# Banded ALiBi attention and a hard-swish MoE on one core: attention of the next batch interleaved with the MoE, masks on GpSimd

## The chip, the cores and the metric

The kernel runs on one core of one Trainium2 chip. The metric is the device time of one execution in microseconds, as the median of several runs. Lower is better.

## The reference, cut to what matters

Inputs are q, k and v of shape (8 batches, 8 heads, 576 positions, 64), and the weights w_in (512 x 2048) and w_out (2048 x 512), all float32.

```
scores = q @ k.T / 8
rel    = pos_q - pos_k
scores = where(0 <= rel < 128, scores - slope[h] * |rel|, -1e9)    # slope[h] = 2 ** -(h+1)
attn   = softmax(scores);  a = attn @ v
x      = a, heads side by side: (8 * 576 = 4608 tokens, 512)
h      = x @ w_in;  g = h * clip(h + 3, 0, 6) / 6;  out = g @ w_out
```

The band is 128 wide, so with tiles of 128 positions a block of queries meets two blocks of keys: its own (the diagonal block, masked on one side) and the one before it (the off-diagonal block, masked on the other side). 576 is four tiles of 128 and one of 64.

## The kernel before, in words

It runs in three stages, one after the other. First it builds 16 bias tiles of 128 x 128 (lines L58 to L77: a diagonal and an off-diagonal one for each head, with the ALiBi slope and a large negative number where the band ends) and loads the weights on SyncE's DMA queue (L86, L90), with a cast to bf16 on VectorE (L87, L91).

Then comes attention: a loop over 8 batches and 4 pairs of heads. For each pair and each of the 5 tiles of positions, six DMAs of 128 x 64 floats bring q, k and v of two heads (L111 to L113), VectorE scales and casts them (L114 to L124), TensorE transposes q and k of both heads together (L126, L128) and VectorE copies the results from PSUM (L127, L129). For each tile of queries and each head there are one or two score matmuls over 64 rows (L144); VectorE adds the bias tile in PSUM (L151), ScalarE takes exp (L153), TensorE multiplies with V (L155). V carries a column of ones, so the sum of the exps comes out beside the product; VectorE takes its reciprocal and multiplies (L160, L161). Both heads are transposed together (L165) and copied into xT (L166), which holds x transposed for all tokens.

Then comes the MoE, over 9 blocks of 512 tokens. In each, over 16 slices of the inner dimension: four matmuls of 512 columns give one 128 x 512 tile of h (L183), ScalarE takes Relu(h / 6 + 0.5) with a bias tile (L188), VectorE takes min with 1 and multiplies by h (L191), and four matmuls of 512 columns add to four output banks (L194). After the 16 slices VectorE copies the four banks out (L200) and SyncE stores them.

A planner of the tile framework orders each engine's instructions ahead of the run, by its own estimate of when operands and buffers are ready, with the program's order as priority. Each engine then runs its list strictly in that order, and a buffer is free again when its last reader is done. PSUM has eight banks; attention uses four kinds of tiles with two buffers each, the MoE four output banks and four banks for h.

## Time and profile before

| | before |
|---|---|
| median of 3 runs | 883.68 us (883.22 to 884.82) |
| profiled execution, span | 881.8 us |
| TensorE matmul busy | 595.5 us (68%) |
| VectorE busy | 577.0 us (65%) |
| ScalarE busy | 245.2 us (28%) |
| GpSimd busy | 5.1 us (1%) |
| DMA | 46.94 MB, 53 GB/s on average |

The profile shows one execution; its span goes from the first to the last instruction, and the time of the runs is 1.9 us above it. Matmuls are pipelined and their ends are modelled, so a busy time of TensorE counts overlapping matmuls' time once but is no measure of how densely they follow each other; start-to-start times are. "Idle before" is the time in which an engine had nothing to do, with the instruction that ended it.

### The profile page before, as it was taken

What the parts mean: (1) busy time and instruction counts of PE and PEld (TensorE: products, weight loads), DVE (VectorE), ACT (ScalarE), POOL (GpSimd) and SP (SyncE); (2) the same over time, 40 slices, a digit from 0 to 9 for tenths busy, and PEclk for the clock granted to TensorE, in tenths of its full rate; (3) what the DMA queues carried; (4) which work ended last, traced back from release to release, by engine and by line L of the source; (5) the groups of instructions that cost most, each with busy time, mean ns of one, the idle gap of its engine ahead of it and who ended that gap; (6) DMA issues with size and microseconds to landing.
All of it is one profiled execution on the core that took longest, in us unless ns stands there. A gap on an engine that the chain in (4) does not pass through costs nothing.

```text
span 881.8 us, 11904 instructions
## 1 busy us (share of the span) xinstructions
PE 595.5 (68%) x2760; PEld 262.3 (30%) x2784; DVE 577.0 (65%) x2939; ACT 245.2 (28%) x721; POOL 5.1 (1%) x24
## 2 busy tenths in 40 slices
PE   0155655565555555655566555555999999999996
PEld 0022222222222222222222222222334333343332
DVE  4577777777777777777777777775354435443543
ACT  0122222222222222222222222222334333433342
POOL 2000000000000000000000000000000000000000
PEclk9999999999999999999999999999999999999999
DMA  6522222222222222222222222221011001100111
GB/s 253 158 49 49 52 54 50 46 52 53 51 47 50 52 53 49 47 52 53 52 45 53 53 52 46 51 46 29 0 48 49 22 26 49 48 34 15 48 48 48
DMA packets 134085, 46.94 MB, mean 53 GB/s; under 512 B 126848, under 2 KB 126848, under 8 KB 133504
## 3 DMA queue, kind: packets, MB, share of 16 engines
q1 hardware_dynamic: 134016, 46.20, 20.2%
q8 instruction: 21, 0.34, 0.2%
q14 instruction: 48, 0.39, 0.2%
HBM read 36.70 MB, written 9.44 MB: 52 GB/s over the span
## 4 chain that ended last, share of the span: by engine, by line
PE 52%; DVE 25%; ACT 9%; issue 7%; DMA 5%; SPq 1%; DVEq 0%; POOL 0%; ACTq 0%; POOLq 0%
PE out_ps L194 15%; PE hT_ps L183 14%; DVE sc_ps L151 9%; ACT exp_sb L153 9%; PE av_ps L155 8%; PE sc_ps L144 6%; DVE qT L127 3%; PE avT_ps L165 3%; PE tps L128 3%; DVE xT L166 3%; PE tps L126 2%; DVE recip L160 2%; DVE vv L105 2%; DVE av_sb L161 2%; DMA tmp<-in_moe_w_out_dram 1%
## 5 line engine op out<-in xcount | busy, mean ns | idle before, releaser
L153 ACT ACTIVATE exp_sb<-sc_ps 128x128 bf16<-128x128 f32 (+1 forms) x576 | 145.0, 264 | 433.2 <-DVE sc_ps L151 364.7
L155 PE MATMUL av_ps<-vv,exp_sb 128*128 128x65 bf16 (+1 forms) x576 | 137.8, 242 | 176.8 <-ACT exp_sb L153 167.1
L151 DVE TENSOR_TENSOR sc_ps<-sc_ps,add_tiles 128x128 f32<-128x128 f32 (+1 forms) x576 | 154.3, 278 | 71.5 <-PE sc_ps L144 59.2
L191 DVE SCALAR_TENSOR_TENSOR gT<-r,hT_ps 128x512 bf16<-128x512 f32 x144 | 98.4, 686 | 141.6 <-ACT r L188 138.2
L144 PE MATMUL sc_ps<-qT,kT 64*128 64x128 bf16 (+1 forms) x576 | 139.2, 273 | 21.3 <-DVE qT L127 11.6
L188 ACT ACTIVATE r<-hT_ps,bias 128x512 f32<-128x512 f32 x144 | 98.9, 687 | 162.2 <-PE hT_ps L183 156.0
L155 PEld LDWEIGHTS <-exp_sb 128*128 128x128 bf16 (+1 forms) x576 | 63.1, 109 | 260.8 <-ACT exp_sb L153 238.9
L183 PE MATMUL hT_ps<-xT,w_in_sb 128*128 128x512 bf16 x565 | 138.9, 382 | 1.1 <-DVE xT L166 0.3
L194 PE MATMUL out_ps<-w_out_sb,gT 128*128 128x512 bf16 x563 | 138.2, 380 | 1.3 <-DVE gT L191 0.9
L161 DVE TENSOR_SCALAR av_sb<-av_ps,recip 128x64 bf16<-128x64 f32 (+1 forms) x320 | 88.3, 276 | 2.4
L183 PEld LDWEIGHTS <-w_in_sb 128*128 128x128 bf16 x576 | 56.8, 99 | 69.1 <-issue 2.2
L126 PE MATMUL tps<-ident,ldb 128*128 128x128 bf16 (+1 forms) x160 | 44.4, 278 | 45.2 <-DMA ldf<-in_k_dram 37.4
L194 PEld LDWEIGHTS <-gT 128*128 128x128 bf16 x576 | 46.4, 97 | 89.2 <-DVE gT L191 51.8
L160 DVE RECIPROCAL recip<-av_ps 128x1 f32<-128x1 f32 (+1 forms) x320 | 50.3, 157 | 33.7 <-PE av_ps L155 30.6
L144 PEld LDWEIGHTS <-kT 64*128 64x128 bf16 x576 | 53.1, 103 | 53.4 <-DVE kT L129 17.5
L128 PE MATMUL tps<-ident,ldb 128*128 128x128 bf16 (+1 forms) x160 | 42.2, 264 | 23.4 <-DVE qT L127 21.4
L165 PE MATMUL avT_ps<-ident,av_sb 128*128 128x128 bf16 (+1 forms) x160 | 44.5, 278 | 11.1 <-DVE av_sb L161 10.6
L166 DVE COPY xT<-avT_ps 128x128 bf16<-128x128 bf16 (+1 forms) x160 | 34.6, 216 | 12.3 <-PE avT_ps L165 8.2
L127 DVE COPY qT<-tps 128x128 bf16<-128x128 bf16 (+1 forms) x160 | 34.5, 216 | 9.9 <-PE tps L126 6.0
L129 DVE COPY kT<-tps 128x128 bf16<-128x128 bf16 (+1 forms) x160 | 34.1, 213 | 4.5 <-PE tps L128 0.5
L126 PEld LDWEIGHTS <-ldb 128*128 128x128 bf16 (+1 forms) x160 | 16.9, 106 | 56.1 <-DVE ldb L117 49.9
L128 PEld LDWEIGHTS <-ldb 128*128 128x128 bf16 (+1 forms) x160 | 16.6, 104 | 50.5 <-DVE ldb L121 38.9
(24 smaller groups left out, 255.7 us busy)
## 6 DMA issues: line engine op xcount, KB each, us to landing
out_dram<-osb SPq DMA_DIRECT2D x36, 256.0 KB, 2.1
ldf<-in_q_dram SPq DMA_DIRECT2D x256, 32.0 KB, 1.8
ldf<-in_k_dram SPq DMA_DIRECT2D x256, 32.0 KB, 1.8
ldf<-in_v_dram SPq DMA_DIRECT2D x256, 32.0 KB, 1.8
tmp<-in_moe_w_in_dram SPq DMA_DIRECT2D x4, 1024.0 KB, 7.8
tmp<-in_moe_w_out_dram SPq DMA_DIRECT2D x16, 256.0 KB, 3.4
ldf<-in_q_dram SPq DMA_DIRECT2D x64, 16.0 KB, 2.0
ldf<-in_k_dram SPq DMA_DIRECT2D x64, 16.0 KB, 2.0
```

The lines of the kernel that those rows point to most:

```text
L126: nc.tensor.transpose(tps[:, :sk], ldb[:sk, 0:2 * D], ident[:sk, :sk])
L128: nc.tensor.transpose(tps[:, :sk], ldb[:sk, 2 * D:4 * D], ident[:sk, :sk])
L144: nc.tensor.matmul(sc_ps[:sk, :sq], lhsT=kT[po:po + D, kslc], rhs=qT[po:po + D, qslc], start=True, stop=True)
L151: nc.vector.tensor_tensor(out=sc_ps[:sk, :sq], in0=sc_ps[:sk, :sq], in1=at, op=ALU.add)
L153: nc.scalar.activation(out=exp_sb[:sk, :sq], in_=sc_ps[:sk, :sq], func=ACT.Exp)
L155: nc.tensor.matmul(av_ps[:sq, :], lhsT=exp_sb[:sk, :sq], rhs=vv[_h][:sk, ds(kt_i * (D + 1), D + 1)], start=first_mm, stop=(kt_i == qt))
L161: nc.vector.tensor_scalar(out=av_sb[:sq, po:po + D], in0=av_ps[:sq, :D], scalar1=recip[:sq, :], scalar2=0.0, op0=ALU.mult, op1=ALU.add)
L165: nc.tensor.transpose(avT_ps[:, :sq], av_sb[:sq, :], ident[:sq, :sq])
L183: nc.tensor.matmul(hT_ps, lhsT=w_in_sb[:, ds(ks * d_ff + ms * 128, 128)], rhs=xT[:, ds(ks * Ntok + nt * NT, NT)], start=(ks == 0), stop=(k ...
L188: nc.scalar.activation(out=r6, in_=hT_ps, func=ACT.Relu, bias=bias3[:, 0:1], scale=1.0 / 6.0)
L191: nc.vector.scalar_tensor_tensor(out=gT, in0=r6, scalar=1.0, in1=hT_ps, op0=ALU.min, op1=ALU.mult)
L194: nc.tensor.matmul(out_ps[sub], lhsT=gT[:, ts(sub, 128)], rhs=w_out_sb[:, ts(ms, d_model)], start=(ms == 0), stop=(ms == n_ms - 1))
```

## The change

Attention is rebuilt and moved between the MoE's matmuls.

- Batch 0 is loaded first. The weights come by eight DMAs that GpSimd issues and that cast to bf16 on the way; nothing else casts them.
- A batch's q, k and v come by 15 DMAs (128 positions x 8 heads x 64), issued one batch ahead as buffers come free. GpSimd casts them to bf16.
- The ALiBi bias is split: within a block, exp(-slope * (q - k)) is a factor of the key, put in as exp's bias (one column per head, for diagonal and off-diagonal blocks), and a factor of the query, which cancels in the normalization. The 1/8 is exp's scale. The bias tiles are gone.
- Scores are taken for key tiles: two key tiles in one PSUM tile of two banks (one bank per head), 256 columns of queries for each, in two steps (`st`) per pair of heads; the second also has the fifth key tile. exp then runs on 256, 128 or 64 elements, and GpSimd zeroes what lies outside the band with affine_select on the exps.
- Normalizing and PSUM copies take whole groups: three reciprocals and three multiplies per pair, one copy of 576 columns per transposed operand.
- The MoE is split into two phases for each 512 tokens: `moe_up` writes all 16 slices of g, and `moe_down`, one block later, multiplies them with w_out, one output bank at a time.
- The main loop runs 10 stages of 16 steps. In stage nt each step has `moe_up` of block nt, `moe_down` of block nt - 1 and two or three of the 37 pieces of attention of batch nt + 1. Batch 0's attention stands alone ahead of the loop; stages 7 to 9 have no attention.

The core of the diff; the lines of the attention and MoE stages shown above are taken out, the sums of the normalization as before.

```diff
...
+    loads = ctx.enter_context(tc.tile_pool(name="loads", bufs=4))
+    casts = ctx.enter_context(tc.tile_pool(name="casts", bufs=2))
+    vpool = ctx.enter_context(tc.tile_pool(name="vpool", bufs=1))
+    qkt = ctx.enter_context(tc.tile_pool(name="qkt", bufs=3))
+    ppool = ctx.enter_context(tc.tile_pool(name="ppool", bufs=4))
+    small = ctx.enter_context(tc.tile_pool(name="small", bufs=4))
+    gpool = ctx.enter_context(tc.tile_pool(name="gpool", bufs=2))
+    rpool = ctx.enter_context(tc.tile_pool(name="rpool", bufs=3))
+    opool = ctx.enter_context(tc.tile_pool(name="opool", bufs=4))
+    ps_sc = ctx.enter_context(tc.tile_pool(name="ps_sc", bufs=1, space=bass.MemoryType.PSUM))
+    ps_av = ctx.enter_context(tc.tile_pool(name="ps_av", bufs=1, space=bass.MemoryType.PSUM))
+    ps_tp = ctx.enter_context(tc.tile_pool(name="ps_tp", bufs=2, space=bass.MemoryType.PSUM))
+    ps_h = ctx.enter_context(tc.tile_pool(name="ps_h", bufs=2, space=bass.MemoryType.PSUM))
+    ps_o = ctx.enter_context(tc.tile_pool(name="ps_o", bufs=1, space=bass.MemoryType.PSUM))
+
+    vbuf = [vpool.tile([128, NQ, H, W], BF16, name=f"vbuf{i}") for i in range(2)]
+    def load(b):
+        got = []
+        for src, nm in ((q, "qf"), (k, "kf"), (v, "vf")):
+            t = loads.tile([128, NQ, H, D], FP32, tag="ld", name=nm)
+            for j in range(NQ):
+                n = min(128, S - j * 128)
+                nc.sync.dma_start(
+                    out=t[:n, j, :, :],
+                    in_=src[b, :, ds(j * 128, n), :].rearrange("h p d -> p h d"))
+            got.append(t)
+        return got
+    first = load(0)
...
+    nc.gpsimd.iota(rel_i, pattern=[[0, 1]], base=0, channel_multiplier=1)
+    nc.vector.tensor_copy(out=rel_f, in_=rel_i)
+    for h in range(H):
+        nc.vector.tensor_scalar(out=bias_d[:, h:h + 1], in0=rel_f, scalar1=-64.0,
+                                scalar2=slopes[h], op0=ALU.add, op1=ALU.mult)
...
+    for ks in range(n_ks):
+        nc.gpsimd.dma_start(out=w_in_sb[:, ks, :], in_=moe_w_in[ts(ks, 128), :])
+    for g in range(4):
+        nc.gpsimd.dma_start(
+            out=w_out_sb[:, ts(g, 4), :],
+            in_=moe_w_out[ds(g * 512, 512), :].rearrange("(m p) d -> p m d", p=128))
+
+    def attention(b):
+        qf, kf, vf = first if b == 0 else load(b)
+        qb = casts.tile([128, NQ, H * D], BF16, name="qb")
+        kb = casts.tile([128, NQ, H * D], BF16, name="kb")
+        vb = vbuf[b % 2]
+        for src, dst in ((qf, qb), (kf, kb)):
+            s = src.rearrange("p j h d -> p j (h d)")
+            nc.gpsimd.tensor_copy(out=dst[:, 0:4, :], in_=s[:, 0:4, :])
+            nc.gpsimd.tensor_copy(out=dst[:LAST, 4, :], in_=s[:LAST, 4, :])
+        nc.gpsimd.tensor_copy(out=vb[:, 0:4, :, 0:D].rearrange("p j h d -> p (j h) d"),
+                              in_=vf[:, 0:4, :, :].rearrange("p j h d -> p (j h) d"))
+        nc.gpsimd.tensor_copy(out=vb[:LAST, 4, :, 0:D], in_=vf[:LAST, 4, :, :])
+        yield
+
+        for hp in range(NP):
+            qkT = []
+            for src, nm in ((qb, "qT"), (kb, "kT")):
+                tp = ps_tp.tile([128, S], BF16, tag="tp", name="tp")
+                for j in range(NQ):
+                    n = min(128, S - j * 128)
+                    nc.tensor.transpose(tp[:, ds(j * 128, n)], src[:n, j, ts(hp, 128)],
+                                        ident[:n, :n])
+                t = qkt.tile([128, S], BF16, tag=nm, name=nm)
+                nc.vector.tensor_copy(out=t, in_=tp)
+                qkT.append(t)
+                yield
+            qT, kT = qkT
+            pt = []
+            avs = small.tile([128, NQ, 2, D], BF16, tag="avs", name="avs")
+            for st in range(2):
+                sc = ps_sc.tile([128, 2, 512], FP32, tag="sc", name="sc")
+                for j in range(2):
+                    kt = 2 * st + j
+                    n = min(256, S - kt * 128)
+                    for e in range(2):
+                        nc.tensor.matmul(sc[:, e, ds(j * 256, n)],
+                                         lhsT=kT[e * D:(e + 1) * D, ts(kt, 128)],
+                                         rhs=qT[e * D:(e + 1) * D, ds(kt * 128, n)],
+                                         start=True, stop=True)
+                if st == 1:
+                    for e in range(2):
+                        nc.tensor.matmul(sc[:LAST, e, 448:512],
+                                         lhsT=kT[e * D:(e + 1) * D, 512:S],
+                                         rhs=qT[e * D:(e + 1) * D, 512:S],
+                                         start=True, stop=True)
+                pp = ppool.tile([128, 2, 2, 256], BF16, tag="p", name="pp")
+                p4 = None
+                if st == 1:
+                    p4 = ppool.tile([64, 2, 64], BF16, tag="p4", name="p4")
...
+                    s4 = sc[:, e, :].rearrange("p (j c) -> p j c", j=2)
+                    nc.scalar.activation(out=pp[:, e, :, 0:128], in_=s4[:, :, 0:128],
+                                         func=ACT.Exp, bias=bias_d[:, h:h + 1], scale=scale)
+                    if st == 0:
+                        nc.scalar.activation(out=pp[:, e, :, 128:256], in_=s4[:, :, 128:256],
+                                             func=ACT.Exp, bias=bias_o[:, h:h + 1], scale=scale)
...
+                dg = pp[:, :, :, 0:128].rearrange("p e j c -> p (e j) c")
+                nc.gpsimd.affine_select(out=dg, in_=dg, pattern=[[0, 4], [1, 128]],
+                                        channel_multiplier=-1, base=0,
+                                        compare_op=ALU.is_ge, fill=0.0)
...
+                pt.append(pp)
+                yield
+                qts = (0, 1) if st == 0 else (2, 3, 4)
+                nq = len(qts)
+                av = ps_av.tile([128, 3, 2, W], FP32, tag="av", name="av")
...
+                        if qt > 0:
+                            src = pt[(qt - 1) // 2][:, e, (qt - 1) % 2, 128:128 + m]
+                            nc.tensor.matmul(av[:m, i, e, :], lhsT=src, rhs=vb[:, qt - 1, h, :],
+                                             start=True, stop=False)
+                        if qt < 4:
+                            src = pt[qt // 2][:, e, qt % 2, 0:128]
+                            nc.tensor.matmul(av[:m, i, e, :], lhsT=src, rhs=vb[:, qt, h, :],
+                                             start=(qt == 0), stop=True)
...
+                    nc.vector.reciprocal(rc[:m, lo:lo + n, :, :], av[:m, lo:lo + n, :, D:W])
+                    nc.vector.tensor_tensor(
+                        out=avs[:m, qts[lo]:qts[lo] + n, :, :],
+                        in0=av[:m, lo:lo + n, :, 0:D],
+                        in1=rc[:m, lo:lo + n, :, :].to_broadcast([m, n, 2, D]),
+                        op=ALU.mult)
+                yield
+            tp = ps_tp.tile([128, S], BF16, tag="tp", name="tp")
+            for j in range(NQ):
+                n = min(128, S - j * 128)
+                nc.tensor.transpose(tp[:, ds(j * 128, n)],
+                                    avs[:n, j, :, :].rearrange("p e d -> p (e d)"), ident[:n, :n])
+            nc.vector.tensor_copy(out=xT[:, hp, ds(b * S, S)], in_=tp)
...
+    def moe_up(nt, ms):
+        if ms == 0:
+            gts[nt] = gpool.tile([128, n_ms, NT], BF16, tag="g", name="g")
+        hps = ps_h.tile([128, NT], FP32, tag="h", name="hps")
+        for ks in range(n_ks):
+            nc.tensor.matmul(hps, lhsT=w_in_sb[:, ks, ts(ms, 128)],
+                             rhs=xT[:, ks, ts(nt, NT)],
+                             start=(ks == 0), stop=(ks == n_ks - 1))
+        r6 = rpool.tile([128, NT], FP32, tag="r6", name="r6")
+        nc.scalar.activation(out=r6, in_=hps, func=ACT.Relu, bias=bias3[:, 0:1], scale=1.0 / 6.0)
+        nc.vector.scalar_tensor_tensor(out=gts[nt][:, ms, :], in0=r6, scalar=1.0, in1=hps,
+                                       op0=ALU.min, op1=ALU.mult)
+
+    def moe_down(nt, step):
+        sub, part = divmod(step, 4)
+        if part == 0:
+            ops[nt, sub] = ps_o.tile([128, d_model], FP32, tag="o", name="ops")
+        for i in range(4):
+            ms = part * 4 + i
+            nc.tensor.matmul(ops[nt, sub], lhsT=gts[nt][:, ms, ts(sub, 128)],
+                             rhs=w_out_sb[:, ms, :], start=(ms == 0), stop=(ms == n_ms - 1))
+        if part == 3:
+            osb = opool.tile([128, d_model], FP32, tag="osb", name="osb")
+            if sub % 2 == 0:
+                nc.scalar.copy(out=osb, in_=ops[nt, sub])
+            else:
+                nc.vector.tensor_copy(out=osb, in_=ops[nt, sub])
+            nc.sync.dma_start(out=out[ds(nt * NT + sub * 128, 128), :], in_=osb)
+
+    for _ in attention(0):
+        pass
+    for nt in range(n_nt + 1):
+        att = list()
+        gen = attention(nt + 1) if nt + 1 < B else iter(())
+        n_units = 1 + NP * 9
+        done = 0
+        for step in range(16):
+            if nt < n_nt:
+                moe_up(nt, step)
+            if nt > 0:
+                moe_down(nt - 1, step)
+            want = (step + 1) * n_units // 16
+            while done < want:
+                done += 1
+                if next(gen, "end") == "end":
+                    done = n_units
+        for _ in gen:
+            pass
```

## Rows read from the trace of the kernel before

**Rows 1.** the span in forty equal slices (tenths busy), granted TensorE clock below

```profile
PE   0155655565555555655566555555999999999996
...
PEclk9999999999999999999999999999999999999999
```

**Rows 2.** busy time by stage: start:end, length, busy (instructions), clock, DMA share, GB/s

```profile
0.00:34.00 34.00, 0.00 (x0) 0.00 (x0) 15.76 (x40) 0.36 (x1) 5.12 (x24) 1.00 0.68 247
34.00:614.50 580.50, 336.42 (x1633) 159.29 (x1634) 441.71 (x2720) 145.94 (x577) 0.00 (x0) 1.00 0.23 50
614.50:872.40 257.90, 256.36 (x1117) 102.11 (x1140) 115.53 (x174) 97.55 (x142) 0.00 (x0) 1.00 0.09 33
872.40:881.80 9.40, 2.76 (x12) 0.91 (x11) 3.95 (x6) 1.37 (x2) 0.00 (x0) 0.92 0.30 112
```

**Rows 3.** the chain that ended last, by engine

```profile
PE 52%; DVE 25%; ACT 9%; issue 7%; DMA 5%; SPq 1%; DVEq 0%; POOL 0%; ACTq 0%; POOLq 0%
```

**Rows 4.** TensorE in attention, in time order: start, length, instruction, [idle before]

```profile
400.41 0.29 PE L144 MATMUL sc_ps<-qT,kT 64*128 64x128 bf16 x2
...
405.11 0.23 PE L155 MATMUL av_ps<-vv,exp_sb 128*128 128x65 bf16 x1 [0.78 <-ACT exp_sb L153]
405.27 0.28 PE L144 MATMUL sc_ps<-qT,kT 64*128 64x128 bf16 x1
405.49 0.24 PE L155 MATMUL av_ps<-vv,exp_sb 128*128 128x65 bf16 x1
...
406.33 0.24 PE L155 MATMUL av_ps<-vv,exp_sb 128*128 128x65 bf16 x1 [0.39 <-ACT exp_sb L153]
406.50 0.29 PE L126 MATMUL tps<-ident,ldb 128*128 128x128 bf16 x1
```

**Rows 5.** the chain at the end, in time order: start, length, what

```profile
865.15 1.73 PE hT_ps L183 x8
866.88 1.89 PE out_ps L194 x8
...
875.40 0.70 DVE osb L200
...
876.12 2.03 DMA out_dram<-osb
```

**Rows 6.** groups by shape, MoE: count, busy us, mean ns, idle before

```profile
L188 ACT ACTIVATE r<-hT_ps,bias 128x512 f32<-128x512 f32 x144 | 98.9, 687 | 162.2 <-PE hT_ps L183 156.0 <-remote 6.2
L191 DVE SCALAR_TENSOR_TENSOR gT<-r,hT_ps 128x512 bf16<-128x512 f32 x144 | 98.4, 686 | 141.6 <-ACT r L188 138.2 <-PE out_ps L194 3.4
...
L183 PEld LDWEIGHTS <-w_in_sb 128*128 128x128 bf16 x576 | 56.8, 99 | 69.1 <-issue 2.2
```

**Rows 7.** groups by shape, attention

```profile
L151 DVE TENSOR_TENSOR sc_ps<-sc_ps,add_tiles 128x128 f32<-128x128 f32 x448 | 125.9, 294 | 66.2 <-PE sc_ps L144 57.7 <-issue 0.4
L153 ACT ACTIVATE exp_sb<-sc_ps 128x128 bf16<-128x128 f32 x448 | 117.0, 277 | 368.4 <-DVE sc_ps L151 300.0 <-DVE ldb L120 60.5
...
L160 DVE RECIPROCAL recip<-av_ps 128x1 f32<-128x1 f32 x256 | 41.8, 163 | 30.7 <-PE av_ps L155 29.6
...
L153 ACT ACTIVATE exp_sb<-sc_ps 128x64 bf16<-128x64 f32 x64 | 14.3, 223 | 48.4 <-DVE sc_ps L151 48.4
```

**Rows 8.** groups by shape, GpSimd

```profile
L77 POOL TENSOR_SCALAR_AFFINE_SELECT add_tiles<-add_tiles 128x128 f32<-128x128 f32 x8 | 2.0, 288 | 0.0
...
masks.py:197 POOL MEMSET ident<- 128x128 bf16 x1 | 0.2, 204 | 0.3 <-POOLq L216 0.3
...
L216 POOL MEMSET const-float32-1.0<- 128x1 f32 x1 | 0.1, 99 | 0.0
```

**Rows 9.** SyncE's DMA queue in attention: start, length of the issue

```profile
306.61 0.38 SPq L112 DMA_DIRECT2D ldf<-in_k_dram  x1
307.08 0.38 SPq L113 DMA_DIRECT2D ldf<-in_v_dram  x1
```

**Rows 10.** TensorE where attention ends and the MoE begins

```profile
614.49 0.59 PE L183 MATMUL hT_ps<-xT,w_in_sb 128*128 128x512 bf16 x1 [0.28 <-DVE xT L166]
```

More of the change, by code (lines that the diff above doesn't have):

```diff
@@ L32 @@
     Ntok = B * S
-    assert d_model == H * D
-    NEG = -1e30
+    assert d_model == H * D and S == 576 and D == 64 and H == 8
     scale = 1.0 / (D ** 0.5)
-    window = 128
-    QT = 128
-    n_qt = (S + QT - 1) // QT
+    NP = H // 2
+    NQ = 5
+    LAST = S - 4 * 128
+    W = D + 1
     slopes = [2.0 ** (-8.0 * (h + 1) / H) for h in range(H)]
+    n_ms = d_ff // 128
+    n_ks = d_model // 128
+    NT = 512
+    n_nt = Ntok // NT
     perm = ctx.enter_context(tc.tile_pool(name="perm", bufs=1))
-    xT = perm.tile([128, (d_model // 128) * Ntok], BF16)
@@ L45 @@
[L45 to L46 removed]
+    xT = perm.tile([128, n_ks, Ntok], BF16)
+    w_in_sb = perm.tile([128, n_ks, d_ff], BF16)
+    w_out_sb = perm.tile([128, n_ms, d_model], BF16)
     ident = perm.tile([128, 128], BF16)
     bias3 = perm.tile([128, 1], FP32)
[L49 to L81 removed]
@@ L83 @@
-    with tc.tile_pool(name="wload", bufs=4) as wl:
-        for kt in range(d_model // 128):
-            tmp = wl.tile([128, d_ff], FP32)
-            nc.sync.dma_start(out=tmp, in_=moe_w_in[ts(kt, 128), :])
-            nc.vector.tensor_copy(out=w_in_sb[:, ts(kt, d_ff)], in_=tmp)
-        for kt in range(d_ff // 128):
-            tmp = wl.tile([128, d_model], FP32)
-            nc.sync.dma_start(out=tmp, in_=moe_w_out[ts(kt, 128), :])
-            nc.vector.tensor_copy(out=w_out_sb[:, ts(kt, d_model)], in_=tmp)
@@ L170 @@
-    NT = 512
-    n_nt = Ntok // NT
-    n_ms = d_ff // 128
-    n_ks = d_model // 128
-    with tc.tile_pool(name="moe", bufs=3) as mp, \
-         tc.tile_pool(name="mps", bufs=1, space=bass.MemoryType.PSUM) as mps, \
-         tc.tile_pool(name="mps2", bufs=4, space=bass.MemoryType.PSUM) as mps2:
-        for nt in range(n_nt):
-            ncol = ds(nt * NT, NT)
-            out_ps = [mps.tile([128, NT], FP32, name=f"out_ps{_i}") for _i in range(n_ks)]
-            for ms in range(n_ms):
-                hT_ps = mps2.tile([128, NT], FP32)
-                for ks in range(n_ks):
-                    nc.tensor.matmul(
-                        hT_ps, lhsT=w_in_sb[:, ds(ks * d_ff + ms * 128, 128)],
-                        rhs=xT[:, ds(ks * Ntok + nt * NT, NT)],
-                        start=(ks == 0), stop=(ks == n_ks - 1))
-                r6 = mp.tile([128, NT], FP32)
-                nc.scalar.activation(out=r6, in_=hT_ps, func=ACT.Relu,
-                                     bias=bias3[:, 0:1], scale=1.0 / 6.0)
-                gT = mp.tile([128, NT], BF16)
-                nc.vector.scalar_tensor_tensor(out=gT, in0=r6, scalar=1.0, in1=hT_ps,
-                                               op0=ALU.min, op1=ALU.mult)
-                for sub in range(n_ks):
-                    nc.tensor.matmul(
-                        out_ps[sub], lhsT=gT[:, ts(sub, 128)],
-                        rhs=w_out_sb[:, ts(ms, d_model)],
-                        start=(ms == 0), stop=(ms == n_ms - 1))
-            for sub in range(n_ks):
-                osb = mp.tile([128, d_model], FP32)
-                nc.vector.tensor_copy(out=osb, in_=out_ps[sub])
-                nc.sync.dma_start(out=out[ds(nt * NT + sub * 128, 128), :], in_=osb)
```

151 lines of the change are left out of this document (45 added, 106 removed).

## The prediction

> **What bounds the kernel now.** I read the forty slices first [rows 1]: TensorE is empty in the first slice, about half busy up to slice 28, full after it; its clock is granted in full throughout, though it is often idle. The stages by windows [rows 2] give the lengths. 0 to 34 us: the weights come in and TensorE does nothing. 34 to 614.5 us: attention, 580.5 us in which TensorE counts 336 us busy, VectorE 442, ScalarE 146. 614.5 to 872.4 us: MoE, 257.9 us, TensorE busy for 256.4. The last 9.4 us are the end. By engine the chain that ended last is half TensorE and a quarter VectorE [rows 3]: in attention no engine is full, work goes round TensorE, VectorE, ScalarE and TensorE again, and the matmul against V waits 0.4 to 0.8 us for each exp [rows 4]. So 580 us are latency and small VectorE instructions; only the 258 us of MoE are TensorE's own. Per matmul of the MoE that is 257.9 / 1152 = 0.224 us (in the chain, eight in a row take 1.73 or 1.89 us [rows 5]).
>
> **The change, part by part.** The span after is a sum of five stretches.
>
> *TensorE in attention.* Per head pair there are 15 transposes, 10 score matmuls and 18 with V: 43, with 2 to 256 columns' worth of work each. The trace has no dense run of short matmuls. From below, two score matmuls of the two heads start almost together, so nearly nothing; from above, 0.16 to 0.22 us from one start to the next where nothing is waited for [rows 4]. The nearest row for a dense run is a weight load, 0.099 us [rows 6], since each short matmul needs one; with a little over it I take 0.107. That is 43 x 0.107 = 4.6 us, and 0.8 us for four changes between 64-row score matmuls and 128-row ones (0.2 each, the upper start-to-start): 5.4 us a pair, 21.6 a batch. Ends: 2.5 and 8.4 us a pair.
>
> *ScalarE.* exp now reads a bias tile. The row with a bias tile is the Relu, 687 ns for 512 elements [rows 6]; the two exp shapes give (277 - 223) / 64 = 0.84 ns an element [rows 7]; so 472 ns for 256, 365 for 128, 311 for 64. The first score tile of a pair has 4 x 472 = 1.9 us, the second 2 x (472 + 365 + 311 + 311) = 2.9 us: 19.2 us a batch, beside 16 Relus (11.0) and two copies (1.4) in a stage: 31.6 us.
>
> *VectorE.* The adds of the bias and most of the small casts and copies go. Left per pair: three copies of 576 elements (0.70 us for 512 [rows 5], so 0.77), three reciprocals (0.16 [rows 7]), multiplies of 256, 256 and 128 elements (at most 294 ns per 128 [rows 7]: 1.5 us): 4.3 us, 17 a batch; with 16 x 0.686 and two copies 30 us a stage.
>
> *GpSimd.* Masks are 2048 elements a pair in 6 instructions, 8192 a batch; casts 7680 a batch. affine_select rows: eight of 128 elements in 2.00 us, 0.25 each; memset 204 ns for 128 elements, 99 for one [rows 8]. An element costs between 0.83 ns (memset's slope) and 2.0 (affine_select without a fixed part). I take (290 - 99) / 127 = 1.5, 0.1 us per instruction: 12 + 12 + 3 = 27 us a batch, ends 16 and 35. A copy with cast on GpSimd has no row; its price here is from these two.
>
> The Trainium skill (GPSIMD Engine Reference, § 3.1) speaks against moving elementwise work there: it has 4497 ns for a two-input add of 2048 elements. No run here shows one. At that 2.2 ns GpSimd would need 38 us a batch, still under a stage's length, and the first casts would be some 3 us later: 500 us in place of 497.
>
> *To the first scores.* Weights (8.39 MB) and batch 0 (3.54 MB, 13,824 pieces of 256 B) now load at once from two queues. At full DMA share the weights run at 247 / 0.68 = 363 GB/s and 256 B pieces at 50 / 0.23 = 217 GB/s [rows 2]: 23 and 16 us, 39 together. Sharing evenly, batch 0 has landed after 33 us, q after 11, k after 22, each 2 us later for landing. k's cast is 2560 x 1.5 ns + 0.2 = 4 us, transposes and copies 1.5: scores start at 30 us. Low end 18 us (weights wait). High end 42: SyncE has shown 128 pieces per 0.47 us [rows 9], that is 51 us for a batch, if 1024 pieces in one instruction go no faster.
>
> *Attention of batch 0.* It stands alone. One buffer of score PSUM means: scores (0.5), all exps (2.4 on average), hand-overs (0.2), next scores: 3.1 us, eight times, 25 us; v's late cast (39 us) hides behind this, as exps of two pairs fit in their buffers. Behind the last exp: masks 1.9, V matmuls 1.1, normalizing 1.2, transposes and copy 1.3: 5.5 us. It ends at 60 us.
>
> *Stage 0* has only the first MoE matmuls (64 x 0.224 = 14.3) and batch 1's attention (21.6): 36 us of TensorE; score tiles of batch 1 may begin 5 us before 60; ScalarE has 30 us and eight hand-overs. I take 34 us, to 94.
>
> *Stages 1 to 6* hold 128 MoE matmuls, 28.6 us, and 21.6 of attention: 50.2. ScalarE 32, VectorE 30, GpSimd 27 are below it, and loads of 3.54 MB take 16 us of DMA time, or at worst 51. TensorE binds. What was hidden behind nothing before, the exp and the mask, is covered by MoE matmuls if the order puts them there. The order is not the program's: a transpose of a later pair stands among V matmuls [rows 4], and the MoE runs 8 + 8 where the program says 4 + 4 [rows 5]. So the planner fills waits with ready work, but with its own guess of durations. For misses I add 8 x 0.3 us, and 1.4 us at the seam, where the next stage's first matmul needs the last pair's transposes while second-phase matmuls are ready: 54 us each, 324, to 418.
>
> *Stages 7 and 8*: 2 x 28.6 = 57.2. *Stage 9*: 64 matmuls 14.3; one output bank, so three turns of a copy (0.70) and two hand-overs, 2.4; last copy and store 0.70 + 2.03 + 0.1 [rows 5]: 19.5.
>
> Sum 60 + 34 + 324 + 57.2 + 19.5 = 494.7 us of span. The profiled execution took as long as the median of the runs within what a page can tell (span 881.8 against 883.68), so I add 1.9: **497 us**.
>
> **Rivals.**
> 1. *Short matmuls stay at 0.2 us.* If score matmuls are mixed singly with MoE matmuls, each pays what [rows 4] show: 43 x 0.195 = 8.4 us a pair, 3 more, 24 pairs in stages 1 to 6 (72 us) and 8 us in stage 0: 577. For it: these are the only cadences seen; against: the rows stand where little was ready, and transposes come in fives. The Trainium skill (TensorEngine Tiling (Array Packing), § Key Properties) says that changing the tiling mode drains TensorE, which would be the cause; the rows agree that such neighbours are not denser than 0.16 us.
> 2. *Waits stay on TensorE.* If the order is the program's, between the scores and their V matmuls lies one MoE step, 1.8 us, against exps 2.4, masks 1.7, hand-overs 0.4: 2.7 us uncovered, eight times, and one tile with no step between: 23 us in place of 3.8 in each of six stages, 115 us; stage 0, with half the cover, 30 us more: 642. Against it: the order seen in [rows 4, 5].
> 3. *No overlap.* All batches share one tensor xT. If MoE matmuls of a stage wait for every write to it, attention runs alone as batch 0 does: 30 + 8 x 30 + 258 + 7 = 535. Against: the MoE of before begins 0.3 us after its wait for the last write to xT [rows 10], which says nothing of parts, so some chance stays.
> 4. *Slower.* GpSimd becomes the bound. Masks and casts are 15,872 elements a batch, one batch a stage. To bring back 883 us seven stages must take (883 - 60 - 57 - 20) / 7 = 107 us, which is from 6.7 ns an element on. The rows stand at 2.0 or less, but for 128 elements of one row, not for a copy with cast or four-dimensional patterns.
>
> **How the numbers follow.** The forecast has 0.60, short matmuls 0.19, waits 0.12, no overlap 0.05, slower 0.03, a bound that I don't see about 0.01. The forecast's own range is 445 to 545 (from below: first scores at 18 us, no misses, 4.8 us a pair; from above: 42 us, 6.7 a pair). For eight in ten I reach over rivals 1 and 3, and leave rival 2 out: 445 to 605. A measurement of this kernel can tell about 0.2% from no change; no case lies near it, so faster 0.96, same 0.01, slower 0.03.
>
> **What would show it.** Right: TensorE nearly full from about 95 us on, first matmul before 20 us and MoE matmuls from about 60 us; one stage every 54 us, eight exps' chain inside it; waits of TensorE for exp or masks small in sum. Rival 1: TensorE full but stages of 66 us. Rival 2: V matmuls waiting for GpSimd, some 20 us a stage. Rival 3: MoE matmuls in blocks without attention between. Rival 4: GpSimd full, its copies over 13 us each. It is wrong if first scores come after 50 us, if a short matmul in a dense run is not near 0.11 us, or if GpSimd is above 1.5 ns by more than half.

## The result and the profile after

The changed kernel takes **477.44 us** (median of 4 runs, 475.87 to 478.99) against 883.62 on the same chip: ratio 0.5399 [0.5386, 0.5412]. The profiled execution spans 477.3 us.

The forty slices of the kernel after, as in [rows 1], with GpSimd and DMA:

```profile
PE   0003775998999999999999999999999999999976
...
POOL 5025644454533622462245225522222222000000
PEclk9999999999799999999999999999999999999999
DMA  8999999500926877669409200000000000101111
GB/s 157 200 205 194 197 198 191 101 0 1 188 66 115 160 146 129 126 143 163 83 23 186 57 23 23 23 22 24 23 23 23 22 23 23 46 22 45 44 45 66
```

TensorE starts at a twelfth of the span and is full from a fifth on: it counts 403 us of 477 busy, 85%, against 595 of 882 before. The windows answer to [rows 2]. They are cut at the first score matmul of a batch (39.2, 79.8, 122.1, 170.7, 217.7, 264.7, 311.7 and 358.7 us in the timeline), with one short stretch, 122.10 to 128.50, by itself; columns: PE, PEld, DVE, ACT, POOL busy (count), clock, DMA share (above 1 where packets' times overlap), GB/s.

```profile
0.00:39.20 39.20, 1.63 (x12) 0.91 (x13) 2.28 (x22) 1.28 (x1) 10.99 (x19) 1.00 1.12 189
39.20:79.80 40.60, 25.53 (x177) 13.15 (x177) 10.57 (x35) 14.79 (x48) 22.21 (x33) 1.00 1.28 196
79.80:122.10 42.30, 38.25 (x255) 17.43 (x256) 20.82 (x53) 24.96 (x65) 20.41 (x32) 0.99 0.27 53
122.10:128.50 6.40, 6.40 (x27) 1.93 (x27) 1.95 (x4) 3.42 (x8) 1.77 (x3) 0.52 1.35 223
...
217.70:358.70 141.00, 135.66 (x901) 63.62 (x900) 67.71 (x162) 76.90 (x199) 46.92 (x84) 1.00 0.23 53
358.70:405.00 46.30, 44.58 (x292) 20.76 (x292) 21.75 (x52) 25.56 (x66) 10.79 (x24) 1.00 0.06 24
405.00:477.30 72.30, 64.94 (x296) 28.72 (x294) 24.41 (x36) 24.08 (x36) 0.00 (x0) 0.99 0.12 44
```

The sixth row is three stages of 47.0 us, TensorE busy for 96% of them; ScalarE, the next, is busy for 55%. Before that lie 122 us in which loading, attention of batch 0 and stage 0 follow one another. The windows don't end where the program's stages do: by 122.1 us TensorE has started 89 MoE matmuls, where the program puts 64 before stage 1, and the last window holds 296, where the program has 320 in stages 7 to 9. The chain by engine [rows 3] now reaches only over about the last 16% of the span:

```profile
PE 15%; issue 1%; DVE 0%; ACT 0%; POOL 0%; POOLq 0%; DVEq 0%
```

The groups by shape that answer to [rows 6 to 8] (count | busy us, mean ns):

```profile
L159 ACT ACTIVATE pp<-sc,bias_d 128x256 bf16<-128x256 f32 x128 | 60.4, 472 | 99.2 <-PE sc L142 54.3 <-PE sc L148 30.1 <-issue 5.9
...
L130 DVE COPY qT<-tp 128x576 bf16<-128x576 bf16 x32 | 14.5, 453 | 45.9 <-PE tp L127 45.8
...
L173 POOL TENSOR_SCALAR_AFFINE_SELECT pp<-pp 128x512 bf16<-128x512 bf16 x64 | 40.6, 634 | 211.2 <-ACT pp L159 106.9 <-issue 103.3 <-POOL vbuf L118 1.0
...
L114 POOL CAST qb<-qf 128x2048 bf16<-128x2048 f32 x8 | 15.1, 1887 | 22.6 <-DMA qf<-in_q_dram 20.3 <-PE tp L127 2.3
```

The records of exp with a bias tile are as long as worked out (472, 361, 313 ns for 256, 128 and 64 elements), but exps in a row start closer together than that, 0.36, 0.25 and 0.20 us apart (ScalarE's timeline in batch 0):

```profile
46.34 0.36 ACT L165 ACTIVATE pp<-sc,bias_o 128x128 bf16<-128x128 f32 x1
46.59 0.31 ACT L167 ACTIVATE pp<-sc,bias_o 128x64 bf16<-128x64 f32 x1
```

So all exps of a score tile take 1.6 us (first tile of a pair) and 2.1 us (second). The GpSimd cast is 1.89 us per 2048 elements, 0.92 ns each; a mask of 512 is 1.24 ns each.

The start, from the timeline of SyncE's queue (with one later row) and of GpSimd (start, length, what):

```profile
0.81 15.76 SPq L80 DMA_DIRECT2D qf<-in_q_dram  x5
16.61 16.06 SPq L80 DMA_DIRECT2D kf<-in_k_dram  x5
32.72 5.97 SPq L80 DMA_DIRECT2D vf<-in_v_dram  x5
...
250.21 4.12 SPq L80 DMA_DIRECT2D kf<-in_k_dram  x5
...
27.14 1.89 POOL L114 CAST qb<-qf 128x2048 bf16<-128x2048 f32 x1 [20.32 <-DMA qf<-in_q_dram]
...
35.91 1.89 POOL L114 CAST kb<-kf 128x2048 bf16<-128x2048 f32 x1 [4.82 <-DMA kf<-in_k_dram]
```

q's five DMAs (4608 pieces) take 15.8 us to issue beside the weights, v's 6, and in a full stage 4. So the first cast waits until 27.1 us. The trace's packets show how the two queues shared: from 4 to 28 us those of the weights moved 129 to 196 GB/s (counted as written, in bf16), those of batch 0 only 14 to 40; from 32 us on, with the weights landed, the 256 B pieces alone moved 181 to 210.

v comes last, and its cast stands ahead of the first masks on GpSimd, so TensorE stands still before its first V matmul:

```profile
42.08 1.90 POOL L116 CAST vbuf<-vf 128x2048 bf16<-128x2048 f32 x1 [3.73 <-DMA vf<-in_v_dram]
...
45.17 0.29 PE L205 MATMUL av<-vbuf,pp 128*128 128x65 bf16 x2 [3.32 <-POOL pp L173]
```

TensorE inside a full stage, as in [rows 4]:

```profile
264.39 0.38 PE L251 MATMUL ops<-w_out_sb,g 128*128 128x512 bf16 x1
264.70 0.39 PE L142 MATMUL sc<-qT,kT 64*128 64x256 bf16 x4
265.03 1.04 PE L235 MATMUL hps<-xT,w_in_sb 128*128 128x512 bf16 x4
...
267.81 0.20 PE L201 MATMUL av<-vbuf,pp 128*128 128x65 bf16 x1
267.85 0.20 PE L205 MATMUL av<-vbuf,pp 128*128 128x65 bf16 x1
267.88 0.19 PE L201 MATMUL av<-vbuf,pp 128*128 128x65 bf16 x1
267.91 0.19 PE L205 MATMUL av<-vbuf,pp 128*128 128x65 bf16 x1
...
269.95 0.27 PE L223 MATMUL tp<-ident,avs 128*128 128x128 bf16 x2
270.06 0.28 PE L127 MATMUL tp<-ident,qb 128*128 128x128 bf16 x2
270.65 0.20 PE L205 MATMUL av<-vbuf,pp 128*128 128x65 bf16 x1 [0.31 <-POOL pp L173]
```

V matmuls in a row start 0.03 to 0.04 us apart, though each record is 0.2 long. Time is lost at the breaks: 0.59 us from the transposes at 270.06 to the V matmul at 270.65, which waits for the mask of the diagonal blocks (L173). Summed from each start to the next over 217.7 to 358.7, the 384 MoE matmuls hold 89 us and the 516 short ones 52 us: 0.233 us each and 4.3 us per pair of heads. (A wait is counted with the matmul before it, so the MoE's 0.233, for 0.216 in a row, holds some 0.5 us of waits per pair.)

The end, from the chain of waits in time order, as in [rows 5]:

```profile
456.72 3.63 PE ops L251 x16
...
460.37 0.59 ACT osb L256
...
473.34 0.69 DVE osb L258
```

Sixteen matmuls take 3.63 us, and between two groups lies one copy out of the only output bank, 0.66 to 0.76 us with its hand-overs; the last store runs to 477.3.

### The profile page after: what moved, and what is told of

It reads as the page before. It is cut to its first block, busy times and chain, and to the rows that moved or that the text cites. A ratio compares the mean times of both kernels' runs of the same rounds, so it can differ in the third digit from the quotient of the medians.

```text
span 477.3 us, 6932 instructions
## 1 busy us (share of the span) xinstructions
PE 403.3 (85%) x2528; PEld 187.2 (39%) x2528; DVE 194.5 (41%) x470; ACT 219.9 (46%) x547; POOL 150.4 (32%) x255
## 3 DMA queue, kind: packets, MB, share of 16 engines
q1 hardware_dynamic: 117696, 37.76, 40.8%
## 5 line engine op out<-in xcount | busy, mean ns | idle before, releaser
L235 PE MATMUL hps<-xT,w_in_sb 128*128 128x512 bf16 x576 | 159.6, 388 | 3.3 <-DVE xT L225 2.1
L239 ACT ACTIVATE r<-hps,bias 128x512 f32<-128x512 f32 x144 | 98.2, 692 | 135.2 <-PE hps L235 135.0
L251 PE MATMUL ops<-w_out_sb,g 128*128 128x512 bf16 x576 | 155.0, 383 | 3.4 <-DVE osb L258 2.0
L240 DVE SCALAR_TENSOR_TENSOR g<-r,hps 128x512 bf16<-128x512 f32 x144 | 97.7, 683 | 114.1 <-ACT r L239 112.8
L173 POOL TENSOR_SCALAR_AFFINE_SELECT pp<-pp 128x512 bf16<-128x512 bf16 x64 | 40.6, 634 | 211.2 <-ACT pp L159 106.9
L159 ACT ACTIVATE pp<-sc,bias_d 128x256 bf16<-128x256 f32 x128 | 60.4, 472 | 99.2 <-PE sc L142 54.3
L251 PEld LDWEIGHTS <-g 128*128 128x128 bf16 x576 | 52.6, 98 | 62.3 <-issue 8.0
L235 PEld LDWEIGHTS <-w_in_sb 128*128 128x128 bf16 x576 | 51.3, 98 | 56.2 <-issue 8.3
L201 PE MATMUL av<-vbuf,pp 128*128 128x65 bf16 (+1 forms) x256 | 44.0, 208 | 5.3 <-DVE avs L214 2.9
L127 PE MATMUL tp<-ident,qb 128*128 128x128 bf16 (+1 forms) x160 | 21.9, 227 | 30.5 <-POOL qb L114 29.1
L214 DVE TENSOR_TENSOR avs<-av,rc 128x256 bf16<-128x256 f32 (+1 forms) x96 | 35.8, 372 | 1.4
L127 PEld LDWEIGHTS <-qb 128*128 128x128 bf16 (+1 forms) x160 | 12.8, 102 | 35.2 <-POOL qb L114 29.1
L142 PEld LDWEIGHTS <-kT 64*128 64x128 bf16 x256 | 10.6, 96 | 34.4 <-issue 19.6
```

The costliest lines, as they stand in the source:

```text
L127: nc.tensor.transpose(tp[:, ds(j * 128, n)], src[:n, j, ts(hp, 128)], ident[:n, :n])
L142: nc.tensor.matmul(sc[:, e, ds(j * 256, n)], lhsT=kT[e * D:(e + 1) * D, ts(kt, 128)], rhs=qT[e * D:(e + 1) * D, ds(kt * 128, n)], start=Tr ...
L159: nc.scalar.activation(out=pp[:, e, :, 0:128], in_=s4[:, :, 0:128], func=ACT.Exp, bias=bias_d[:, h:h + 1], scale=scale)
L173: nc.gpsimd.affine_select(out=dg, in_=dg, pattern=[[0, 4], [1, 128]], channel_multiplier=-1, base=0, compare_op=ALU.is_ge, fill=0.0)
L201: nc.tensor.matmul(av[:m, i, e, :], lhsT=src, rhs=vb[:, qt - 1, h, :], start=True, stop=False)
L214: nc.vector.tensor_tensor(out=avs[:m, qts[lo]:qts[lo] + n, :, :], in0=av[:m, lo:lo + n, :, 0:D], in1=rc[:m, lo:lo + n, :, :].to_broadcast( ...
```

## The experiments

Where no ratio is given, the time is that of a single execution. All but the last three alter the changed kernel.

**1. Without overlap.** The main loop runs all attention first; the MoE's pools take the PSUM banks of attention afterwards.

```diff
-    for _ in attention(0):
-        pass
+    for b in range(B):
+        for _ in attention(b):
+            pass
+    att_ps.close()
```

> The rebuilt attention of all eight batches first, then the two-phase MoE, which takes over attention's PSUM banks and so cannot start before attention ends. What it tells: how much of the gain is the rebuilt attention and how much the overlap. If the overlap carries a good part (my theory): attention keeps the pace that batch 0 has in the changed kernel, 8.75 us a pair of heads, so 39 + 8 x 35 + 5 = 324 us, and 1152 matmuls at 0.216 us plus an end of 6 us: about 580 us. Rival, the overlap carries nearly all and the rebuilt attention alone is as slow as before (580 us for eight batches): over 850 us. Rival, the rebuilt attention alone would do: under 500 us.

Measured 597.45 us, near the theory's 580. Attention runs from 39.2 us to the first MoE matmul at 329.4: 36 us a batch, against 580.5 / 8 = 73 in [rows 2]. So of the 406 us gained some 286 come from attention rebuilt, and 120 from its place beside the MoE.

**2. All attention first in the program**, with the buffers and banks as changed, so that the planner may overlap (the lines above without `att_ps.close()`).

> The changed kernel with one alteration in the order of the program: the attention of all eight batches is written ahead of all MoE work, in place of a piece of attention after each of 16 MoE steps; buffers and PSUM banks as in the changed kernel, and the planner may still place an instruction anywhere. Theory (the overlap comes from the order in the program, which the planner alters only over a short reach): it runs like the kernel in which attention and MoE cannot overlap, 560 to 600 us. Rival (the planner finds the overlap by itself): 475 to 500 us.

Measured 495.58 us: the rival was right. The first MoE matmul still starts at 51.9 us. The planner finds the overlap over hundreds of instructions; the written interleaving is worth 18 us here or less. How much of that is the order stays open: the clock was at 0.5, the lower of its two levels, from 211.7 to 256.1 us, which can cost up to half of these 44 us (columns as above):

```profile
222.00:272.00 50.00, 37.60 (x271) 19.71 (x274) 15.23 (x48) 20.35 (x66) 24.70 (x42) 0.66 0.28 72
```

**3. TensorE in program order.** Every matmul and transpose is kept where the program has it.

```diff
+    def matmul(*a, **k):
+        return tc.keep_in_program_order(mm(*a, **k))
...
```

> Every instruction of TensorE is pinned behind the one before it in the program; the other engines keep the planner's freedom. Rival 2 of the prediction priced this order: 2.7 us of uncovered exp and mask per score tile, 23 us in place of the few in each of six stages and 30 us more in stage 0, about 620 to 640 us. If the planner's order matters little, because the pieces of attention were already spread over the steps by hand: 477 to 500 us.

Measured 576.86 us. The wait of TensorE for the diagonal mask over the whole span (us, times, longest), in this kernel and then in the changed one:

```profile
PE av L33 <- POOL pp L180: 63.1, 64, 5.6
```

```profile
PE av L205 <- POOL pp L173: 11.6, 25, 3.3
```

64 times is once per score tile. Rival 2's mechanism is real: this wait alone grew by 51.5 us, and the planner's order avoids most of it. Neither figure expected came: 576.86 lies under the 620 to 640 of rival 2 and far above 500. Nor are the 99 us all waits. TensorE's clock was granted at 0.935 on the mean, for 0.992 in the changed kernel's profile; at two levels, 1 and 0.5, that is some 75 us at the lower one, which can have cost up to 37 us:

```profile
PEclk9999998777989999998799889977998899899999
```

**4. No masks.** The affine_selects on the exps are left out (so the output has the terms outside the band).

```diff
-                nc.gpsimd.affine_select(out=dg, in_=dg, pattern=[[0, 4], [1, 128]],
...
```

> Leaves out all of GpSimd's masks, so what lies outside the band is not zeroed; the rest is the changed kernel. Theory, TensorE binds stages 1 to 6: these stages keep 47 to 48 us each, and only batch 0's attention and stage 0, which wait for masks on TensorE, get shorter, 5 to 12 us together: 465 to 472 us. Rival, attention's own chain (scores, exps, masks, V matmuls) paces the stages and the MoE only fills it: 8 score tiles a batch each lose 1 to 1.9 us, so stages of 36 to 40 us and a time of 415 to 435 us.

Measured 435.59 us, at the upper end of the rival's range, but its stages of 36 to 40 did not come. Attention of batch 0 takes 34.2 us for 40.6, stage 0 35.9 for 42.3, later stages 42.1 to 43.1 for 47.0 to 48.6. So the theory, full stages kept at 47 to 48, is out, and the rival holds in part: a full stage is TensorE's work (run 5) and waits for masks, one after the other. The masks cost 42 us though GpSimd is a third busy. Waits of TensorE's weight loads in three stages, first the changed kernel, then without masks:

```profile
PEld L205 <- POOL pp L173: 10.0, 24, 0.6
```

```profile
PEld L187 <- ACT pp L159: 11.2, 30, 0.6
```

This wait doesn't vanish: it moves to the exp. Weight loads run ahead of the matmuls, so this column is no path time; the stages are. On the matmuls themselves the masks show: in three full stages the starts of V matmuls that come more than 0.25 us after the start before them (42) sum to 16.1 us, and without masks (19) to 5.6.

**5. Half of the second phase** (8 of 16 matmuls per output tile left out).

```diff
-        for i in range(4):
+        for i in (0, 3):
```

> Leaves out half of the second-phase MoE matmuls (two of four in each step, so the output sums only half of the inner dimension). Nine stages have 32 matmuls of 0.216 us less, 6.9 us of TensorE each. If TensorE's own work sets stages 1 to 6: each falls from 47 to about 40, stages 7 to 9 fall too, 62 us in all: 410 to 420 us. Rival, attention's chain with the masks paces stages 1 to 6, as leaving the masks out suggested: only stages 7 to 9 fall, 21 us: 453 to 460 us. In between, both at once: a stage cannot go under the 42 us that stage 0 takes with half of the MoE's work, so 6 x 5 + 21 = 51 us: about 426 us.

Measured 421.37 us, just above the theory's range. Three full stages take 40.8 us on the mean (first scores at 199.4 and 321.8 us) for 47.0: 6.2 us of the 32 x 0.216 = 6.9 removed, with the clock at its lower level twice for 3.4 us within them. TensorE is the path of the full stages: what it need not do there shortens them, as do the mask waits that run 4 takes out (4.9 us).

**6. Each V matmul twice** (a repeat in the same accumulation).

```diff
-                for i, qt in enumerate(qts):
+                for i, qt in [x for p in enumerate(qts) for x in (p, p)]:
```

> Each matmul of the exps with V is done twice (the second time over, with the same result): 18 more a pair, 576 in all. What it tells is the price of a short matmul in this order. At the dense start-to-starts seen in the changed kernel (0.034 to 0.05 us, 0.15 for the four of a pair with 64 stationary columns): 1.2 us a pair more, 32 pairs, 38 us: 505 to 520 us. At the prediction's 0.107: 62 us, 540 us. Rival 1 of the prediction, 0.2 us: 115 us, 590 us.

Measured 507.03 us, in the theory's range: 29.6 us for 576 more, 0.051 us each. Full stages take 51.3 us for 47.0, 0.060 for each of 72. Rival 1's 0.2 is out, and the 0.107 of the prediction is about twice too high for V matmuls.

**7. Weights late.** The weights' DMAs stand behind the casts of batch 0's q and k.

```diff
+        if b == 0:
+            with tc.issue_after(last_cast.ins):
+                for ks in range(n_ks):
...
```

> The eight weight DMAs are queued on GpSimd behind the cast of batch 0's q instead of ahead of it. In the changed kernel the loads of q, k and v of batch 0 are issued over 38 us (5 DMAs in 16 us beside the weights, in 6 us without them) and the first scores come at 39 us, 9 later than predicted. Theory, the weights hold up batch 0's load: first scores at 18 to 22 us and the whole time shorter by that, 457 to 462 us. Rival, the late weights now hold up the first MoE matmuls or batch 1's loads: first scores early, but the time within 5 us of 477. Rival, the load is slow by itself (1024 pieces per DMA): first scores still after 35 us.

Measured 478.62 us, ratio 0.5408 [0.5394, 0.5422]. The first scores come at 16.9 us, 22 earlier, and nothing is gained, as the first rival had it. The queue and GpSimd show where it went:

```profile
16.42 24.57 SPq L80 DMA_DIRECT2D qf<-in_q_dram  x5
...
25.95 0.33 POOL L189 TENSOR_SCALAR_AFFINE_SELECT p<-p 64x128 bf16<-64x128 bf16 x1
45.72 1.89 POOL L108 CAST qb<-qf 128x2048 bf16<-128x2048 f32 x1 [19.44 <-DMA qf<-in_q_dram]
```

Now batch 1's q loads beside the weights, and its cast stands on GpSimd ahead of batch 0's masks: 19.4 us in which no mask runs.

**8. Off-diagonal masks on VectorE**, as a product with a 0/1 tile.

```diff
-                    nc.gpsimd.affine_select(out=of, in_=of, pattern=[[0, 4], [-1, 128]],
...
+                    nc.vector.tensor_tensor(out=of, in0=of, op=ALU.mult,
+                                            in1=m_off.to_broadcast([128, 4, 128]))
```

> The off-diagonal masks go to VectorE, as a multiplication by a tile of zeros and ones built once; the diagonal ones stay on GpSimd, so a tile's masks run side by side. Leaving all masks out made a stage 4.8 us shorter and the start 12.8 us. Theory, TensorE waits for the masks' latency: with half of it gone stages are 44 to 45 us and the start some 5 us shorter, 455 to 463 us. Rival, VectorE's multiplications stand behind its other work (Relu products of 0.69 us) or share an SBUF port with GpSimd, and the masks are no earlier: 473 to 485 us.

Measured 476.30 us, ratio 0.5390 [0.5373, 0.5407], the changed kernel's within the interval. The rival was right. Batch 0's attention is shorter, 36.8 us for 40.6, but stage 0 is longer, 45.4 for 42.3. Full stages take 46.5 us; the weight loads' wait for the diagonal mask is what it was, over three stages:

```profile
PEld L208 <- POOL pp L178: 9.9, 24, 0.6
```

This speaks for the end of a tile's first mask, and against GpSimd's load, as what counts; run 11 tests it. A gain of a few microseconds may be hidden: the mean clock of the four executions was 0.980 to 0.992, in the changed kernel 0.992 to 1.000.

**9. The start put in order.** w_in behind batch 0's q and k casts, w_out behind batch 1's, and batch 1's casts behind the masks of batch 0's third pair.

```diff
+        if b == 1:
+            pin.enter_context(tc.issue_after(mask2[0].ins))
...
+        if b < 2:
+            with tc.issue_after(cast.ins):
+                weights(b)
```

> The start in another order: w_in's DMAs behind the casts of batch 0's q and k, w_out's behind those of batch 1, and batch 1's casts pinned on GpSimd behind the masks of batch 0's third pair (with the weights late and nothing else, first scores came at 17 us, but GpSimd then stood from 26 to 48 us before batch 1's first cast, whose load was held up, with the masks of batch 0 behind it). Theory, DMA traffic and that place in GpSimd's list are all that held the start: first scores at 17, stage 0 from about 58 us in place of 80, 452 to 459 us. Rival, batch 1's load still lands too late for stage 0: 468 to 478 us.

Measured **450.56 us**, ratio 0.5102 [0.5093, 0.5110]. That is a little under the 452 to 459 expected. First scores at 16.7, 54.5, 97.1, 141.3 us; later stages stay at 47.1. With 7 this shows that the start was worth 27 us, and that loads, casts and masks had to be put in order together. In the profiled executions 25 us are gained by the end of stage 0 and 4 in stage 1, which takes 44.1 us for 48.6; the changed kernel's low clock falls into that stage.

**10. Next pair's q and k transposes early**, on top of 9.

```diff
+        yield from qk(0)
         for hp in range(NP):
...
+                if st == 1 and hp + 1 < NP:
+                    yield from qk(hp + 1)
```

> The 450.6 us kernel with the q and k transposes of the next pair written ahead of the second score tile of this pair, so that they no longer stand behind V matmuls that wait for a mask. Theory (in the opening, with no MoE work to fill TensorE, the pair rate of 8.75 us comes from that order): pairs of batch 0 at about 7 us, first scores of batch 1 from 54.5 to about 48 us, stage 0 a few us shorter as well, stages 2 to 6 unchanged at 47 us because TensorE is full there: 440 to 445 us. Rival (the pair rate is set by the one PSUM tile of scores and the chain scores, exps, mask, V matmuls through it): pairs stay at 8 us or more, 448 to 452 us.

Measured **432.75 us**, ratio 0.4892 [0.4884, 0.4900], more than expected, and not as expected. The first pair of batch 0 falls from 12.4 to 5.2 us, the next two only from 8.4 and 8.7 to 8.1 and 7.9, and the fourth grows from 8.3 to 10.9; stage 0 from 42.6 to 36.9; the full stages from 47.1 to 45.6, where I had expected nothing. What shortens them is not shown: the starts of V matmuls more than 0.25 us behind sum to 19.0 us in three stages, 16.3 in run 9. The timeline from the second pair of batch 0 on:

```profile
22.31 0.61 PE L161 MATMUL sc<-qT,kT 64*128 64x256 bf16 x4 [2.22 <-ACT p L188]
...
24.58 0.56 PE L161 MATMUL sc<-qT,kT 64*128 64x256 bf16 x4 [0.85 <-ACT pp L181]
...
26.76 0.80 PE L139 MATMUL tp<-ident,qb 128*128 128x128 bf16 x5
...
30.36 0.61 PE L161 MATMUL sc<-qT,kT 64*128 64x256 bf16 x4 [0.36 <-DVE avs L235]
```

The second pair's tiles are 2.3 us apart, but the third pair's transposes still run behind the second's V matmuls, at 26.8. Why they aren't placed earlier was not tried.

**11. Diagonal exps of both heads first**, on top of 9.

```diff
+                for e in range(2):
+                    h = 2 * hp + e
+                    nc.scalar.activation(out=pp[:, e, :, 0:128], in_=s4s[e][:, :, 0:128],
+                                         func=ACT.Exp, bias=bias_d[:, h:h + 1], scale=scale)
                 for e in range(2):
...
```

> The 450.6 us kernel with the exps of both heads' diagonal blocks ahead of those of the off-diagonal blocks, so that the first mask of a score tile can start one exp (0.36 to 0.67 us) sooner, while the others still run. Theory (what the masks cost a stage, 4.8 us of 47, is the time that the first V matmuls wait for the diagonal mask, 0.4 to 0.6 us at 8 breaks a stage): most of the breaks shorten, stages 2 to 6 go from 47 to 43 to 45 us and the opening by a few us: 430 to 440 us. Rival (TensorE waits for the last mask of the tile, or the planner places the V matmuls by its own model of times, so that an earlier mask gives nothing): stages stay at 46.5 to 47 us, 447 to 452 us.

Measured 439.50 us, ratio 0.4969 [0.4962, 0.4977]. The full stages go from 47.1 to 45.3 us; batch 0's attention does not shorten (39.8 for 37.8). In three of them the starts of V matmuls more than 0.25 us behind sum to 12.1 us, 16.3 in run 9, so it is the wait for masks that shrinks. The late start of the diagonal mask is thus 1.8 of the near 5 us that masks cost a stage, less than the 2 to 4 expected; on what the opening hangs this run doesn't show.

**12. Both.**

> Both alterations of the two kernels before on the 450.6 us kernel: next pair's q and k transposes ahead of the second score tile (alone 432.8 us, 17.8 gained, pairs of batch 0 every 8.0 us, stages 45.6) and both diagonal exps first (alone 439.5 us, 11.1 gained, pairs 8.3, stages 45.3). Theory (they shorten different waits: the first takes transposes out from behind the V matmuls, the second lets the diagonal mask start sooner): the gains add, 421 to 425 us, pairs of batch 0 near 7.5 us, stages 2 to 6 near 44 us. Rival (both shorten the same wait of TensorE for a mask, one by work put into it and one by an earlier end): hardly better than the first alone, 429 to 433 us, stages 45 us or more.

Measured **425.54 us**, ratio 0.4812 [0.4804, 0.4821], the fastest here: 25.0 of the 28.9 us that the two gained alone, between theory and rival and nearer the theory. Three full stages:

```profile
175.10:308.20 133.10, 127.45 (x888) 62.32 (x900) 66.18 (x162) 77.78 (x199) 47.88 (x84) 1.00 0.31 67
```

That is 44.4 us a stage. By the times, most of what they shorten is different, a small part the same. The waits before V matmuls agree: 12.8 us in three stages, as with run 11's alteration alone, which run 10's did not shorten.

## Why the prediction was right

The time is 4% below the forecast and inside its range, but two steps were off by more than that, with opposite signs: the start came late and the full stages were short. The mechanism, TensorE as the bound of stages in which attention fills in between MoE matmuls, was right; that the two errors nearly cancel is luck.

- *First scores* at 39.2 us, forecast 30 (18 to 42). The step that failed is the even sharing. In total the loads were nearly as forecast: weights and batch 0 had landed after 43 us, forecast 41 with the landing. But until the weights had landed at 30.6 us, batch 0's pieces moved only 14 to 40 GB/s beside them; alone they moved 181 to 210, near the forecast's 217. So q had landed after 30 us and k after 37, not after 13 and 24. SyncE's high bound (36 times 0.47 us for 4608 pieces, 17 us [rows 9]) was near the 15.8 and 16.1 us beside the weights and far above the 4 to 6 us without them. TensorE's first matmul came at 29.1 us, not before 20.
- *Attention of batch 0*: 40.6 us, forecast 30. The exps of a score tile take less than forecast, 1.6 and 2.1 us for 1.9 and 2.9, but pairs come every 8.7 to 11.8 us, not 6.2: the forecast had no place for the next pair's transposes, which stand behind V matmuls that wait for masks. Run 4 (34.2 us without masks) and the first pair in run 10 (5.2 us) show the two parts; what keeps the middle pairs at 8 us stays open. Nor does v's late cast hide, as the forecast had it: TensorE waits 3.3 us before the first V matmul. *Stage 0*: 42.3 us, forecast 34, in the same way. Together the start is 28 us late: 122.1 for 94. Some 5 us of that are no delay: 25 MoE matmuls more than the forecast's 64 are done by then.
- *Full stages*: 48.6 and 47.0, forecast 54. TensorE binds, as forecast (runs 5 and 6). The step that was mis-sized is its price in attention: V matmuls cost 0.05 us (run 6) or 0.04 in a row, not 0.107, and the 43 short matmuls of a pair with their breaks 4.3 us, or 4.8 with the waits counted with the MoE's, against 5.4 and 0.95 of misses. The prediction named "not near 0.11 us" as what would make it wrong: that came true, and moved the time only by the part that waits did not take back. The breaks of 0.3 to 0.6 us at a change to V matmuls are what the forecast's misses stood for; at 3.8 us a stage these were too low, as run 4 takes 4.9 us out of a stage with the masks alone. From 122.1 to 405 us the stages gave back 41 us of 324.
- *Stages 7 to 9*: 72.3 us, forecast 76.7, but with 296 MoE matmuls for 320. With the 24 done before, 5.2 us, the end would be 77.5 us, nearly as forecast: 0.216 us per matmul for 0.224 [rows 5] gave back 2.6 us, and the rest, copies and the last store above all, took 8.4 us for 5.0.
- The sum by windows: +28 - 41 - 4.4 = -17, which is 477.3 less 494.7. With each matmul counted in the stage that the program gives it, the start is 23 us late and the end 1 us.
- *ScalarE and VectorE*: the exps' records as forecast, but closer together; VectorE's copies of 576 elements 0.45 us for 0.77. In the three full stages ScalarE is busy 25.6 us a stage (forecast 32) and VectorE 22.6 (30), below TensorE as forecast.
- *GpSimd*: 150.4 / 8 = 19 us a batch, forecast 27 (16 to 35). The Trainium skill (GPSIMD Engine Reference, § 3.1) has 4497 ns for a two-input add of 2048 elements, 2.2 ns each; the cast here, of one input, takes 0.92 and the mask 1.24, so its figure doesn't carry over to these.
- *Rivals.* 1 (0.2 us each) is out by run 6. The Trainium skill (TensorEngine Tiling (Array Packing), § Key Properties) has a drain at a change of tiling mode; the rows leave room for a tenth of a microsecond at the change (0.31 us from the MoE matmul at 264.39 to the scores at 264.70, for 0.216 between two of the MoE) and for none inside the four scores, which take 0.33 together. The forecast had 0.2 for a change. 2 (program order) exists, but has to be forced. 3 (no overlap) is out: MoE matmuls start at 52.65 us, within batch 0's attention, so waits on xT go by its parts. 4 (GpSimd the bound) is out at 32% busy, yet its masks cost 42 us (run 4); run 8 speaks for their latency as the cause.

## What to carry to other kernels

When two kinds of work are interleaved, price the short instructions by their spacing in a dense run and the waits by the number of breaks, not by the length of a record. An engine that is a third busy can still cost a tenth of the time, if each tile passes through it between two steps of the full engine: shorten its first result, not its load. Moving a load earlier pays only if everything behind it on the same queues (the next batch's loads, casts, masks) is moved with it.
